# Attention, gated projection and product block on one core: the RMS root of the first five units by ScalarE's square root, reciprocal and two Newton steps

## The chip, the core and the metric

The kernel runs on one core of a Trainium2 chip. The metric is the device time of one execution in microseconds; three executions of the kernel before took 1012.33, 1013.52 and 1014.37 us, with a median of 1013.52.

## What is computed

Three blocks follow each other. Keys and values are averaged over eight positions each before the attention; the result is normalised by the root of its mean square, gated, and multiplied out; a second block multiplies two projections.

```
k_p, v_p = mean of k, v over 8 positions each          # batch 4, heads 8, seq 576, dim 64
attn = softmax(q @ k_p.T / sqrt(64));  x = attn @ v_p   # then 2304 tokens x 512
rms = sqrt(mean(x * x, axis=-1) + 1e-06)
xn  = x / rms * rms_g
x   = (silu(xn @ w_gate) * (xn @ w_val)) @ w_out        # d_ff 1536
out = ((x @ w_a) * (x @ w_b)) @ w_out2
```

The five weight matrices come in 64-bit floating point and are turned into 32-bit on the chip, by integer and bit instructions. Most products are made of three passes, of a high and a low part of each factor.

## The kernel before

The 2304 tokens are nine attention units of 256 tokens, 0 to 8. The first block runs over five tiles of 512, 256, 512, 512 and 512 tokens (TILES1); units 0 and 1 make the first tile, unit 2 the second, units 3 and 4 the third. While a tile is multiplied, the units of the next are worked on beside it. The order of the first two tiles' work is written out by hand (the tables FIRST and SECOND; a sign before a step says behind which work a step may stand), and a scheduler places the instructions of each engine in a queue that the engine then works in order. From the last tile on, the order is the program's own.

A unit's steps that matter here, with their lines:

- Scores: q is transposed (L298, copied by ScalarE at L307), multiplied by K (L318), and the maximum found and subtracted by VectorE (L327, L328). Two PSUM banks, tag "att", go round among these steps, so a step waits until the bank's last reader is done. Keys and values are pooled by VectorE (L189) or GpSimd (L180, L183) from tiles loaded at L169 and L171, two buffers.
- Values: the exponentials are transposed (L367, copied by ScalarE at L374) and multiplied by V (L420 for units 0 and 1, L399 for the others). ScalarE copies the result to x with the factor of the RMS weight (L423, L403), and squares it (L425, L406, L409).
- Mean square: TensorE sums the squares by a product with ones into a tile of 128x4 (L434 for units 0 and 1, L445 for 2 to 4).
- Root, `narrow_rsqrt` (L454), units 0 to 4: VectorE makes `a`, half the mean square, a first guess by integer operations (`start_newton`, L478 to L485), three Newton steps (L491 to L493), and a diagonal matrix of the 256 roots in two pieces (L464). TensorE spreads it by a product with ones (`spread`, L472, "rb" in the rows), VectorE scales x with it (L529). Units 5 to 8 use another path, with wide tiles at the same lines L478 to L493.
- Split: ScalarE casts x to its high part xh (L635), VectorE subtracts to the low part xl (L636).

The first block's 36 weight parts of 512 KB each are loaded by SyncE (L566, L571) into four staging tiles "st", converted by ScalarE (`begin`, L589 and L590), VectorE (`sign`, L596, L599) and GpSimd (`end`, L606), whose addition frees the staging tile; then split into wh by ScalarE (L620) and wl by GpSimd or VectorE (L621). The first tile's projections are L799, its Silu L807, its gated product L813, and the product with w_out L670. For the other tiles these are L649, L1239, L1247 and L670 or L662. Gates have one PSUM bank, values another.

Of the kernel before, what the change touches and what calls it, by code (L numbers as in the profile page):

```python
# [8 lines left out]
F32 = mybir.dt.float32  # L9
# [4 lines left out]
AF = mybir.ActivationFunctionType  # L14
ALU = mybir.AluOpType
AX = mybir.AxisListType

P = 128
# [45 lines left out]
def attention_moe_moe2(  # L64
# [14 lines left out]
    nc = tc.nc  # L79
    B, H, S, D = q.shape  # L80
    NT, DM = out.shape
# [19 lines left out]
    const = attn.enter_context(tc.tile_pool(name="const", bufs=1, side="right"))  # L101
# [10 lines left out]
    for t0, n in starts(TILES1):  # L112
        x2d[t0] = dr.tile([DM, n], F32, tag=f"x2_{t0}", name=f"x2_{t0}")

    ident = const.tile([P, P], F32, tag="ident", name="ident")
# [6 lines left out]
        out=mask, in_=mask, pattern=[[P, NV], [-SP, H]], compare_op=ALU.is_ge,  # L122
# [3 lines left out]
        out=mask, in_=mask, pattern=[[-P, NV], [SP, H]], compare_op=ALU.is_ge,  # L126
# [7 lines left out]
    vp = const.tile([P, NV, D], F32, tag="vp", name="vp")  # L134
    nc.gpsimd.memset(vp, 0.0)
    gneg = const.tile([P, KD], F32, tag="gneg", name="gneg")

    VH, VL, VM = {}, {}, {}

# [218 lines left out]
    def value_steps(u, dest):  # L358
        t0, n = u * UNIT, UNIT
        box, eT = {}, {}  # L360
# [81 lines left out]
        def sum_tokens():  # L442
            box["sums"] = att_bank(f"sq_{u}")
            for i in range(NS):
                nc.tensor.matmul(  # L445
                    box["sums"][:, 2 * i:2 * i + 2],
                    box["ss"][:, i * P:(i + 1) * P],
                    ones.bitcast(F32)[:, :2],
                    start=(i == 0),
                    stop=(i == NS - 1),  # L450
                )
            narrow_rsqrt()

        def narrow_rsqrt():  # L454
            m = 2 * NS
            a = sm_p.tile([P, m], F32, tag="ba", name=f"ba_{u}")
            r = sm_p.tile([P, m], F32, tag="br", name=f"br_{u}")
            y = sm_p.tile([P, m], F32, tag="by", name=f"by_{u}")
            start_newton(box["sums"][:, :m], a, r)
            for _ in range(3):  # L460
                newton_step(a, r, y)
            diag = sm_p.tile([P, n], F32, tag="nr", name=f"dg_{u}")
            for i in range(NS):
                nc.vector.tensor_scalar_mul(  # L464
                    diag[:, i * P:(i + 1) * P], ident, r[:, 2 * i:2 * i + 1]
                )
            box["diag"] = diag

        def spread():
# [7 lines left out]
        def start_newton(src, a, r):  # L477
            nc.vector.tensor_scalar(  # L478
                out=a, in0=src, scalar1=0.5 / DM, scalar2=0.5e-6, op0=ALU.mult, op1=ALU.add
            )  # L480
            nc.vector.tensor_scalar(
                out=r.bitcast(I32), in0=a.bitcast(I32), scalar1=1, scalar2=None,
                op0=ALU.logical_shift_right,
            )
            nc.vector.tensor_scalar(  # L485
                out=r.bitcast(I32), in0=r.bitcast(I32), scalar1=-1.0,
                scalar2=float(0x5F3759DF - 0x400000), op0=ALU.mult, op1=ALU.add,
            )

        def newton_step(a, r, y):  # L490
            nc.vector.tensor_mul(y, r, r)  # L491
            nc.vector.tensor_mul(y, y, a)
            nc.vector.scalar_tensor_tensor(  # L493
                out=r, in0=y, scalar=1.5, in1=r, op0=ALU.subtract, op1=ALU.mult
            )
# [37 lines left out]
        if u * UNIT < TILES1[0]:  # L533
            return steps + [narrow_rsqrt, scale]
# [663 lines left out]
    for idx, (ph, t0, n) in enumerate(work):  # L1198
# [26 lines left out]
        for f, cols, last, ahead, own in jobs:  # L1225
            m = cols.stop - cols.start
# [94 lines left out]
```

## Time and profile before

| what | value |
|---|---|
| profiled execution, its own time | 1014.52 us |
| its span, first to last instruction | 1012.8 us |
| mean granted TensorE clock | 0.990 |
| TensorE (PE) busy | 976.4 us, 96% |
| VectorE (DVE) busy | 610.0 us, 60% |
| ScalarE (ACT) busy | 452.0 us, 45% |
| GpSimd (POOL) busy | 402.9 us, 40% |
| activation table loads | 16, 1283 ns each |

Busy time is an average over stages: TensorE's idle time lies almost wholly before 130 us, where the weights are converted and the first tile is made. In the rows, PE is TensorE, PEld its weight loads, DVE VectorE, ACT ScalarE, POOL GpSimd and SPq SyncE's queue; L12 is line 12 of the kernel before, and "out<-in" names tiles of the program.

### The profile page before, as it was taken

How to read it: one execution, taken by the hardware profiler on the slowest of the kernel's cores; microseconds unless marked ns; L12 is line 12 of the kernel's file. 1: busy time of each engine (PE TensorE's matmuls, PEld its weight loads, DVE VectorE, ACT ScalarE, POOL GpSimd, SP SyncE). 2: the span in 40 equal slices, each digit the busy share in tenths (PEclk: the TensorE clock that was granted, in tenths of full speed). 3: DMA queues.
4: the chain of work that ended last, by engine and by line, in shares of the span. 5: the costliest groups of instructions: out<-in, count | busy, mean ns of one | idle time of the engine just before them, and what ended most of it. 6: DMA issues, size and time to landing. Idle time of an engine off the chain costs nothing.

```text
span 1012.8 us, 13575 instructions
## 1 busy us (share of the span) xinstructions
PE 976.4 (96%) x4920; PEld 842.3 (83%) x4920; DVE 610.0 (60%) x966; ACT 452.0 (45%) x849; POOL 402.9 (40%) x324
## 2 busy tenths in 40 slices
PE   4878999999999999999999999999999999999998
PEld 3766666789888888888888899999999999888886
DVE  6898966766636565566338669667766665232321
ACT  3854662454644445544445545443444344331211
POOL 6476673434343354344356701433443333410000
PEclk8799999999999999999999999999999999999999
DMA  8556543330100001000121143434434445643431
GB/s 230 159 167 206 171 130 107 115 89 1 43 11 11 1 30 34 1 1 1 42 62 43 42 148 130 131 125 146 147 125 136 126 136 184 193 146 116 146 112 67
DMA packets 82946, 101.55 MB, mean 100 GB/s; under 512 B 24128, under 2 KB 63296, under 8 KB 82880
## 3 DMA queue, kind: packets, MB, share of 16 engines
q1 hardware_dynamic: 82736, 100.55, 32.0%
q8 instruction: 39, 0.64, 0.3%
q14 instruction: 27, 0.22, 0.1%
q10 hardware_dynamic: 144, 0.13, 0.0%
HBM read 73.93 MB, written 26.74 MB: 99 GB/s over the span
## 4 chain that ended last, share of the span: by engine, by line
PE 81%; DVE 11%; DMA 3%; issue 2%; ACT 2%; SPq 0%; DVEq 0%; ACTq 0%
PE o L1120 15%; PE X L1019 14%; PE v L649 10%; PE g L649 10%; PE acc L662 9%; PE Y L1019 7%; PE acc L670 3%; PE Z L1019 3%; PE xT L399 2%; PE v L799 2%; PE g L799 1%; PE sc L318 1%; DVE wf L596 1%; DVE wf L599 1%; DVE kp L189 1%
## 5 line engine op out<-in xcount | busy, mean ns | idle before, releaser
L621 POOL TENSOR_TENSOR wl<-wf,wh 128x512 fp32r<-128x512 f32 x144 | 196.6, 1373 | 230.7 <-ACT wh L620 221.0
L620 ACT CAST wh<-wf 128x512 fp32r<-128x512 f32 x156 | 94.8, 619 | 70.2 <-PE v L649 30.2
L1098 DVE TENSOR_TENSOR hl<-hf,hh 128x768 fp32r<-128x768 f32 x36 | 34.5, 963 | 95.0 <-ACT hh L1097 95.0
L1120 PE MATMUL o<-woh,hl 128*128 128x512 f32 x216 | 85.8, 397 | 0.0
L1120 PE MATMUL o<-woh,hh 128*128 128x512 f32 x216 | 85.0, 394 | 0.0
L1120 PE MATMUL o<-wol,hh 128*128 128x512 f32 x216 | 84.7, 392 | 0.0
L606 POOL TENSOR_TENSOR w<-w,st 128x512 int32<-128x512 int32 x24 | 31.9, 1329 | 116.8 <-DVE w L599 115.6
L649 PE MATMUL v<-xh,wl 128*128 128x512 f32 (+1 forms) x192 | 72.6, 378 | 1.6 <-DVE ht L1247 1.6
L649 PE MATMUL g<-xh,wl 128*128 128x512 f32 (+1 forms) x192 | 72.4, 377 | 0.0
L649 PE MATMUL v<-xh,wh 128*128 128x512 f32 (+1 forms) x192 | 69.9, 364 | 0.0
L649 PE MATMUL v<-xl,wh 128*128 128x512 f32 (+1 forms) x192 | 69.8, 364 | 0.0
L649 PE MATMUL g<-xh,wh 128*128 128x512 f32 (+1 forms) x192 | 69.8, 364 | 0.0
L649 PE MATMUL g<-xl,wh 128*128 128x512 f32 (+1 forms) x192 | 69.8, 363 | 0.0
L1097 ACT CAST hh<-hf 128x768 fp32r<-128x768 f32 x36 | 29.8, 834 | 87.9 <-PE o L1120 81.5
L670 PE MATMUL acc<-ht,wf 128*128 128x256 f32 (+1 forms) x208 | 67.0, 463 | 1.7 <-DVE xf L529 1.3
L606 POOL TENSOR_TENSOR wf<-wf,st 128x512 int32<-128x512 int32 x36 | 52.9, 1475 | 38.2 <-DVE wf L599 16.6
L1247 DVE TENSOR_TENSOR ht<-ht,v 128x512 f32<-128x512 f32 (+1 forms) x48 | 29.6, 617 | 60.3 <-PE v L649 56.2
L1239 ACT ACTIVATE ht<-g 128x512 f32<-128x512 f32 (+1 forms) x48 | 26.1, 544 | 74.3 <-PE g L649 73.7
L1027 ACT COPY p<-X 128x384 f32<-128x384 f32 x36 | 17.2, 478 | 90.2 <-PE X L1019 90.2
L662 PE MATMUL acc<-hh,wl 128*128 128x512 f32 x144 | 56.4, 392 | 0.0
L662 PE MATMUL acc<-hl,wh 128*128 128x512 f32 x144 | 56.1, 390 | 0.0
L662 PE MATMUL acc<-hh,wh 128*128 128x512 f32 x144 | 56.1, 389 | 0.0
(210 smaller groups left out, 2704.5 us busy)
## 6 DMA issues: line engine op xcount, KB each, us to landing
hf<-h SPq DMA_DIRECT2D x36, 384.0 KB
st<-in_moe_w_out_dram SPq DMA_DIRECT2D x24, 512.0 KB
h<-u SPq DMA_DIRECT2D x36, 192.0 KB
h<-p SPq DMA_DIRECT2D x36, 192.0 KB
st<-in_moe_w_gate_dram SPq DMA_DIRECT2D x12, 512.0 KB
st<-in_moe_w_val_dram SPq DMA_DIRECT2D x12, 512.0 KB
st<-in_moe_w_a_dram SPq DMA_DIRECT2D x12, 512.0 KB
st<-in_moe_w_b_dram SPq DMA_DIRECT2D x12, 512.0 KB
```

The lines of the kernel that those rows point to most:

```text
L606: nc.gpsimd.tensor_tensor(out=bits, in0=bits, in1=low, op=ALU.add)
L620: nc.scalar.copy(wh, wf[ph, f, i])
L621: (nc.vector if boot["alt"] else nc.gpsimd).tensor_sub(wl, wf[ph, f, i], wh.bitcast(F32))
L649: nc.tensor.matmul(bank[:, :n], w[:, c, :], x[:, c, cols], start=(i == 0), stop=(i == 3 * KD - 1),)
L662: nc.tensor.matmul(accs[c][:, cols], w[:, c, :], x[:, :n], start=(f == 0 and i == 0 and cols.start == 0), stop=(f == NF - 1 and i == 2),)
L670: nc.tensor.matmul(accs[c][:, cols], wf[0, f, 2][:, c, :], ht[:, :cols.stop - cols.start], start=(f == 0 and cols.start == 0), stop=(f == ...
L799: nc.tensor.matmul(bank[:, :n], w[:, c, :], x[:, c, cols], start=(c == 0 and i == 0), stop=(c == KD - 1 and i == len(terms) - 1),)
L1019: nc.tensor.matmul(dst[:, :HALF], w[:, c0 + c, :], x[:, c, :], start=(start and i == 0), stop=(stop and i == 5), skip_group_check=True,)
L1097: nc.scalar.copy(hh, hf)
L1098: nc.vector.tensor_sub(hl, hf, hh.bitcast(F32))
L1120: nc.tensor.matmul(accs[i], x[:, sub], y, start=(f == 0 and j == 0), stop=(f == NF - 1 and j == 2),)
L1247: nc.vector.tensor_mul(ht[:, :m], ht[:, :m], vb[:, :m])
```

## The change

The start by integer operations and the first of three Newton steps go. ScalarE takes the square root of the mean square (with a constant tile for the 1e-6), VectorE its reciprocal, and two refining steps follow, of which the first is written with other signs. The diagonal is made by ScalarE. ScalarE needs the table of the square root for this, so it loads that table before the root and Silu's or the exponential's again after it.

```diff
@@ -134,6 +134,8 @@
     gneg = const.tile([P, KD], F32, tag="gneg", name="gneg")
+    eps = const.tile([P, 2], F32, tag="eps", name="eps")
+    nc.gpsimd.memset(eps, 1e-6)
@@ -456,14 +458,23 @@
             y = sm_p.tile([P, m], F32, tag="by", name=f"by_{u}")
-            start_newton(box["sums"][:, :m], a, r)
-            for _ in range(3):
-                newton_step(a, r, y)
+            src = box["sums"][:, :m]
+            nc.scalar.activation(out=y, in_=src, func=AF.Sqrt, scale=1.0 / DM, bias=eps[:, 0:1])
+            nc.vector.tensor_scalar(
+                out=a, in0=src, scalar1=0.5 / DM, scalar2=0.5e-6, op0=ALU.mult, op1=ALU.add
+            )
+            nc.vector.reciprocal(r, y)
+            nc.vector.tensor_mul(y, r, r)
+            nc.vector.scalar_tensor_tensor(
+                out=y, in0=y, scalar=-1.0, in1=a, op0=ALU.mult, op1=ALU.mult
+            )
+            nc.vector.scalar_tensor_tensor(
+                out=r, in0=y, scalar=1.5, in1=r, op0=ALU.add, op1=ALU.mult
+            )
+            newton_step(a, r, y)
             diag = sm_p.tile([P, n], F32, tag="nr", name=f"dg_{u}")
             for i in range(NS):
-                nc.vector.tensor_scalar_mul(
-                    diag[:, i * P:(i + 1) * P], ident, r[:, 2 * i:2 * i + 1]
-                )
+                nc.scalar.mul(diag[:, i * P:(i + 1) * P], ident, r[:, 2 * i:2 * i + 1])
             box["diag"] = diag
```

Since the scheduler places instructions anew, other work moves too. In the changed kernel, lines behind the edit are larger by 2 to 11 (L364 to L458 by 2, L470 and later by 11). Three places:

ScalarE's queue at unit 0's root and unit 1's squares, before (ef is the transposed exponential, xf x, sq a square, st_1_0 and st_1_1 staged weights):

```order
L374 COPY ef_0_367<-eT_0_364 128x256
L374 COPY ef_1_393<-eT_1_390 128x256
L374 COPY ef_2_411<-eT_2_408 128x256
L589 ACTIVATE wf_0_1_435<-st_1_0_246 128x512
L590 ACTIVATE st_1_0_246<-st_1_0_246 128x512
L423 ACTIVATE xf_296<-xT_0_414,gneg 128x256
L425 ACTIVATE sq_0_418<-xT_0_414 128x256
L374 COPY ef_3_423<-eT_3_420 128x256
L423 ACTIVATE xf_296<-xT_1_425,gneg 128x256
L374 COPY ef_4_450<-eT_4_447 64x256
L589 ACTIVATE wf_0_1_497<-st_1_1_274 128x512
```

and with the change:

```order
L376 COPY ef_0_369<-eT_0_366 128x256
L462 ACT_TABLE_LOAD
L462 ACTIVATE by_373<-sq_299,eps 128x4
L376 COPY ef_1_392<-eT_1_389 128x256
L376 COPY ef_2_410<-eT_2_407 128x256
L600 ACTIVATE wf_0_1_434<-st_1_0_248 128x512
L601 ACTIVATE st_1_0_248<-st_1_0_248 128x512
L425 ACTIVATE xf_298<-xT_0_413,gneg 128x256
L477 ACTIVATE dg_383<-ident,br_372 128x128 x2
L427 ACTIVATE sq_0_417<-xT_0_413 128x256
L376 COPY ef_3_422<-eT_3_419 128x256
L425 ACTIVATE xf_298<-xT_1_424,gneg 128x256
```

The load, the root and the diagonal stand between unit 1's copies and squares, and the begin of st_1_1 (wf_0_1_497 before) has moved behind all of unit 1's squares.

VectorE's queue at the end of unit 1's root, before (ba, br and by are the narrow tiles, wf weights under conversion, ht the gated product):

```order
L599 SCALAR_TENSOR_TENSOR wf_0_1_528<-st_1_2_356,wf_0_1_528 128x512
L493 SCALAR_TENSOR_TENSOR br_473<-by_474,br_473 128x4
L596 TENSOR_SCALAR wf_0_2_562<-wf_0_2_562 128x512
L491 TENSOR_TENSOR by_474<-br_473 128x4
L599 SCALAR_TENSOR_TENSOR wf_0_2_562<-st_2_0_433,wf_0_2_562 128x512
L492 TENSOR_TENSOR by_474<-by_474,ba_472 128x4
L493 SCALAR_TENSOR_TENSOR br_473<-by_474,br_473 128x4
L813 TENSOR_TENSOR ht<-ht,v 128x256
L491 TENSOR_TENSOR by_474<-br_473 128x4
L492 TENSOR_TENSOR by_474<-by_474,ba_472 128x4
L493 SCALAR_TENSOR_TENSOR br_473<-by_474,br_473 128x4
L464 TENSOR_SCALAR dg_487<-ident,br_473 128x128 x2
```

and with the change:

```order
L463 TENSOR_SCALAR ba_471<-sq_412 128x4
L466 RECIPROCAL br_472<-by_473 128x4
L467 TENSOR_TENSOR by_473<-br_472 128x4
L468 SCALAR_TENSOR_TENSOR by_473<-by_473,ba_471 128x4
L471 SCALAR_TENSOR_TENSOR br_472<-by_473,br_472 128x4
L502 TENSOR_TENSOR by_473<-br_472 128x4
L503 TENSOR_TENSOR by_473<-by_473,ba_471 128x4
L504 SCALAR_TENSOR_TENSOR br_472<-by_473,br_472 128x4
L824 TENSOR_TENSOR ht<-ht,v 128x256
L607 TENSOR_SCALAR wf_0_1_524<-wf_0_1_524 128x512
L540 TENSOR_TENSOR xf_298<-xf_298,rb_486 128x4x256
L610 SCALAR_TENSOR_TENSOR wf_0_1_524<-st_1_2_358,wf_0_1_524 128x512
```

The whole root stands in one piece, and the conversion of st_1_2 and st_2_0, which stood between its links, comes behind it.

VectorE's queue where unit 2 is scaled, before (kp and vp are pooled keys and values, m and e maximum and exponent of the scores, rb the spread root):

```order
L189 TENSOR_REDUCE kp_1593<-kv_4_1596 72x64 x2
L327 TENSOR_REDUCE m_1485<-sc_0_1488 128x4
L327 TENSOR_REDUCE m_1485<-sc_1_1493 128x4
L328 TENSOR_TENSOR e_1367<-sc_0_1488,m_1485 128x288
L328 TENSOR_TENSOR e_1367<-sc_1_1493,m_1485 128x288
L189 TENSOR_REDUCE kp_1593<-kv_3_1610 72x64
L529 TENSOR_TENSOR xf_1210<-xf_1210,rb_1510 128x4x256
```

and with the change:

```order
L191 TENSOR_REDUCE kp_1586<-kv_4_1589 72x64 x2
L191 TENSOR_REDUCE kp_1586<-kv_3_1603 72x64 x2
L329 TENSOR_REDUCE m_1478<-sc_0_1481 128x4
L329 TENSOR_REDUCE m_1478<-sc_1_1486 128x4
L330 TENSOR_TENSOR e_1363<-sc_0_1481,m_1478 128x288
L330 TENSOR_TENSOR e_1363<-sc_1_1486,m_1478 128x288
L824 TENSOR_TENSOR ht<-ht,v 128x512
L191 TENSOR_REDUCE vp<-kv_2_1608 128x64
L540 TENSOR_TENSOR xf_1206<-xf_1206,rb_1503 128x4x256
```

Both pools of kv_3 now stand ahead of the subtraction that frees the bank for the spread root, and the first pool of kv_2 ahead of the scaling.

## Rows read from the trace of the kernel before

**Rows 1.** Busy time by stage, core 0: stretch, length, engines, TensorE clock, DMA.

```profile
34.00:62.40 28.40, 21.16 (x106) 17.61 (x103) 25.12 (x49) 16.27 (x34) 16.28 (x14) 0.82 0.53 162
...
72.00:94.00 22.00, 17.82 (x68) 13.45 (x67) 21.80 (x24) 11.34 (x20) 17.79 (x14) 0.92 0.69 216
...
260.00:1012.80 752.80, 746.12 (x3730) 658.65 (x3728) 413.52 (x646) 317.08 (x591) 262.45 (x199) 1.00 0.28 89
```

**Rows 2.** Chain of waits, 0 to 80 us: start, length, engine, tile, line.

```profile
39.63 1.02 PE rb L472 x2
...
43.90 0.16 DVE ba L478
...
45.14 0.96 DVE kp L189
46.10 1.20 DVE xl L636 x2
...
47.38 0.33 DVE wf L596
...
54.17 0.04 DVE dg L464
...
57.55 1.14 DVE xf L529
...
59.37 3.03 DVE xl L636 x2
```

**Rows 3.** Who waited for whom, TensorE, whole span: total us, times, longest.

```profile
PE qT L298 <- DMA q<-in_q_dram: 10.5, 1, 10.5
PE v L799 <- DVE ht L813: 4.2, 2, 2.8
...
PE rb L472 <- DVE e L328: 1.0, 1, 1.0
```

**Rows 4.** VectorE, lines L492 and L341: duration ns minimum, median, maximum.

```profile
L492 DVE TENSOR_TENSOR by<-by,ba x15: 146/162/1211, 35.8 to 249.7; 128x4 f32<-128x4 f32 x15
...
L341 DVE RECIPROCAL sum<-sum x11: 184/239/253, 19.0 to 430.0; 128x16 f32<-128x16 f32 x7, 128x8 f32<-128x8 f32 x4
```

**Rows 5.** Instructions in order of time, ScalarE, 222 to 225 us: start, length.

```profile
222.71 1.28 ACT L1239 ACT_TABLE_LOAD   x1
224.01 0.38 ACT L1239 ACTIVATE ht<-g 128x256 f32<-128x256 f32 x1
```

**Rows 6.** ScalarE, line L403: duration ns minimum, median, maximum.

```profile
L403 ACT ACTIVATE xf<-xT,gneg x28: 467/474/489, 138.8 to 458.8; 128x256 f32<-128x256 f32 x28
```

**Rows 7.** Instructions in order of time, ScalarE, 24 to 70 us.

```profile
33.46 1.04 ACT L374 COPY ef<-eT 128x256 f32<-128x256 f32 x3
...
37.03 0.68 ACT L589 ACTIVATE wf<-st 128x512 f32<-128x512 f32 x1
...
43.04 1.14 ACT L635 CAST xh<-xf 128x512 fp32r<-128x512 f32 x2
```

**Rows 8.** Instructions in order of time, GpSimd, 24 to 70 us.

```profile
41.72 1.28 POOL L606 TENSOR_TENSOR wf<-wf,st 128x512 int32<-128x512 int32 x1 [3.08 <-ACT st L590]
...
66.71 1.37 POOL L606 TENSOR_TENSOR wf<-wf,st 128x512 int32<-128x512 int32 x1 [3.20 <-DVE wf L599]
```

**Rows 9.** SyncE's queue in order of time, 20 to 75 us.

```profile
43.03 0.34 SPq L571 DMA_DIRECT2D st<-in_moe_w_out_dram  x1
...
55.73 0.39 SPq L566 DMA_DIRECT2D st<-in_moe_w_val_dram  x1
```

**Rows 10.** Instructions in order of time, VectorE, 182 to 188 us.

```profile
184.14 0.68 DVE L636 TENSOR_TENSOR xl<-xf,xh 128x512 fp32r<-128x512 f32 x1
```

**Rows 11.** Instructions in order of time, ScalarE, 222 to 262 us.

```profile
241.35 0.38 ACT L1239 ACTIVATE ht<-g 128x256 f32<-128x256 f32 x1 [0.68 <-PE g L649]
...
249.16 0.39 ACT L1239 ACTIVATE ht<-g 128x256 f32<-128x256 f32 x1 [2.74 <-PE g L649]
```

**Rows 12.** Who waited for whom, 66 to 140 us.

```profile
ACT wf L589 <- DMA st<-in_moe_w_val_dram: 5.2, 3, 2.1
```

## Prediction

> **What bounds the kernel now.** I read the page's busy shares first (TensorE leads), then the busy time by stage, the chain of waits, and who waits for whom. Time is to be had only where TensorE isn't busy: the table by stage shows it busy for 746.12 of the last 752.8 us, but for only 21.16 of the 28.4 us from 34 to 62.4, with a mean granted clock of 0.82, and for 17.82 of 22 us from 72 to 94 [rows 1]. In both stretches VectorE is nearly full (25.12 of 28.4, 21.80 of 22). Units 0 and 1 lie in the first of them; units 2 to 4 lie where TensorE is nearly full.
>
> From 43.9 to 62.4 us the chain of waits runs almost wholly on VectorE: unit 1's root starts at 43.90, the low part of x for unit 0 is made at 46.10, unit 1's diagonal comes at 54.17, the scaling of its x at 57.55, and the low part of that is whole at 62.4 [rows 2]. So some fourteen instructions on tiny tiles, spread through VectorE's queue, hold up half of the first tile for 10.3 us. Besides, TensorE waits 4.2 us for gated products that stand behind the weights' conversion in that queue, and 1.0 us, in unit 2, for an attention subtraction [rows 3].
>
> **The change part by part.** *VectorE.* Per unit, three start instructions, nine of Newton's and two diagonal ones go (14); one affine, one reciprocal and six products come (8). A small one takes 0.16 us at the median but up to 1.2, the reciprocal of a similar tile 0.18 to 0.25 [rows 4]; in the stretch at hand the long ones lie beside a GpSimd instruction and end with it. I take 0.2 each with the gap to the next, so twelve links (2.4 us) become eight (1.6), without the blocks. What stands between the links counts for more: the order rows show unit 1's links now in one piece.
>
> *ScalarE.* Per unit a square root and two diagonal instructions come, and seven table loads in all (one for units 0 and 1 together, two each for units 2, 3 and 4). A load takes 1.28 us, and the Silu after it starts 0.02 later [rows 5], so 1.3 each and 9.1 in all. The Trainium skill, page "ScalarE: Activation LUTs", section "What ACT_TABLE_LOAD costs", gives 2.66 us for a switch, load and drain. These rows show no such drain; by the page unit 0 would come 1.4 us later than below and the sum would be -2.4 instead of -3.8. The root and the diagonal have no row on ScalarE; below them lies 0.31 (the pitch of its copies of 256 columns [rows 7]) or less, above them 0.47, its copy with a scale from a tile [rows 6]. With fewer columns than either, I take 0.25 for four and 0.3 for 128.
>
> *Unit 0.* The root's table load stands behind the first of three score copies, which start at 33.46 [rows 7]: 33.8 + 1.3 + 0.25 = 35.35. On VectorE seven links and a conversion step of 0.33 to 0.4 [rows 2] follow: 37.2. Diagonal 0.6: 37.8; TensorE's spread 1.02 and the scaling 1.14 [rows 2]: 40.0, where they end at 41.9 now. ScalarE casts x at 40.4 instead of 43.04 [rows 7]. VectorE pools two K chunks at about 1.0 each [rows 2] and starts the low part at 42.1 instead of 46.10: -4.0.
>
> *Unit 1.* Its last sums of squares now stand behind twelve projections: 45.4, which is 1.5 later than now. Root 45.7; the chain 1.6 and one GpSimd instruction of up to 1.3 beside it: 47.3 to 48.6, I take 48. Silu's table load and Silu end at 47.4, before the chain does, and so cost nothing; were the root later they would add up to 1.7. Diagonal, spread and scaling end at 50.7 instead of 58.7; the cast waits for two conversion pairs on ScalarE (51.4), and the low part is whole at 53.1 instead of 62.4: -9.3.
>
> *Weights.* These pay for it. ScalarE's part of the weight that it begins at 37.03 now [rows 7] moves behind unit 1's squares, to 42.2; VectorE's and GpSimd's follow, so the addition of 41.72 [rows 8] comes at 45.2. Each addition frees one of four staging tiles, so the load that SyncE issues at 43.03 [rows 9] goes out at 46.5; the one of 55.73 at about 59.5, since in SyncE's queue a V load that waits for a K pooling now stands ahead of it. But these were early: the tile loaded at 43.03 is added only at 66.71 [rows 8], because VectorE was in arrears. Following VectorE's new queue, that addition comes at about 61, and the three after it 4 to 5 us before their present places. From there the four staging tiles pace the conversion as they do now.
>
> TensorE can get ahead only by the smaller of 9.3 (x) and 4 to 5 (weights): I take **-4.5** for the start. The rest of the 9.3 becomes new waiting for weights at 60 to 75.
>
> *Units 2 to 4.* In unit 2 the pools of two more K chunks stand ahead of the subtraction that TensorE's spread waits for (1.0 now [rows 3]), and a V pool ahead of the scaling. VectorE's low part ends at 184.8 now [rows 10]; with the two pools ahead it comes at 186.9, some 0.2 after TensorE needs it, and the spread waits 1.6 instead of 1.0: together **+0.7**. In unit 3 two loads and the wait for the diagonal make the Silu of 241.35 [rows 11] about 0.6 late, and delayed copies hold a PSUM bank: 0 to +0.6; I take 0, since the product that needs this Silu comes four microseconds later. In unit 4 two loads and the root (2.85) meet ScalarE's idle 2.74 before the Silu of 249.16 [rows 11]: 0. What VectorE saves there brings nothing, as TensorE doesn't wait for it. The fill of a 128x2 tile by GpSimd at the program's start is hidden by the 10.5 us in which TensorE waits for the first q [rows 3]; without that cover it is below an addition's 1.28 [rows 8].
>
> Sum: -4.5 + 0.7 = **-3.8 us**. The profiled execution took 1014.52 (span 1012.8 and 1.7 around it), so 1010.7; it lies 1.0 above the median of 1013.52, and against the median this is **1009.7**.
>
> **The rivals.**
> *The gain is twice that.* If the weights keep up, TensorE follows x: -9.3, of which unit 2 takes 0.7 and waits on gated products some 1.1: 1006. For it: VectorE, which converts the weights, is relieved too, and gated products move ahead of conversion steps in its queue (4.2 us of waits [rows 3]). Against: VectorE's 21.80 of 22 us from 72 to 94 [rows 1].
> *Nothing is left.* ScalarE, working in order, is the new wait: in units 3 and 4 Silu stands behind a load, a root, a diagonal that VectorE must finish first, and another load. If the chain there meets GpSimd's instructions as the long ones do now (1.2 instead of 0.16 [rows 4], twice), each Silu comes 1.5 to 2 us late, and TensorE, with one bank for gates, stops for it: +3 to +4 on the -3.8, so 1013. Beside this stands the rule of the same page, section "Table sets: the hidden batching unit", to group calls by set, which the change goes against. Against it: ScalarE's idle 2.74 [rows 11].
> *Slower.* The staging ring decides. If TensorE's path up to 94 us is set not by VectorE's arrears but by when the four tiles come free, the 3.5 us by which the load of 43.03 slips pass through every later load: 1013.5 + 3.5 = 1017. It decides from the point where ScalarE waits for a load longer than VectorE works off its queue. For it: ScalarE does wait for weight loads between 66 and 140 [rows 12]. Against: the tile loaded at 43.03 lies until 66.71 [rows 8, 9].
> *The clock.* A mean of 0.82 over 28.4 us [rows 1] is 10 us at the lower level of 1.2 GHz. If TensorE's waiting for unit 1 keeps it there 10 us longer, the matmuls at 53 to 63 take up to twice their time; since weights bind until about 70, that is 2 us of the gain at most, inside the forecast's own bounds.
>
> **How the numbers follow.** Forecast 0.50, twice the gain 0.17, nothing left 0.21, slower 0.12. About 0.2% (2 us) is what a measurement of this kernel can tell from no change. By its bounds (start -3 to -6, units 2 to 4 from 0 to +2) the forecast runs from 1007 to 1012.5, and a tenth of it lies within 0.2%. Faster: 0.45 + 0.17 = 0.62; same: 0.05 + 0.20 = 0.25; slower: 0.12 and 0.01 of the third case, 0.13. The range that holds 8 in 10 takes in the upper half of the double gain and the case of nothing left: 1005 to 1014.5.
>
> **What would show it.** Right: unit 1's diagonal at about 48 instead of 54, the low part of its x whole near 53, 23 table loads of 1.28 with nothing behind them, the addition of 66.71 near 61, TensorE busier from 34 to 62, and the stretch after 260 as long as now. Wrong: VectorE idle after 46 for want of loads (the staging ring), TensorE waiting for Silu near 240 and 250 (ScalarE), or the addition at 66 or later.

## The result and the profile after

The changed kernel takes 1021.66 us (median of 5 runs, 1017.75 to 1023.55) where the kernel before takes 1013.52: the ratio is 1.0073, with an interval of [1.0059, 1.0088]. It is slower by 7.4 us by the ratio and by 8.1 by the medians, where 3.8 us less was forecast, and it lies above the range. The ratios, here and below, leave out two executions that lie far off all others (1956 us in E1, 1565 us of the kernel before). The profiled execution took 1021.66, its span is 1019.6 and its mean granted clock 0.986. Profiles are compared below with the one of the kernel before, which lies 1.0 above its median, so they show the loss some 1 us too small.

Busy time by stage, the changed kernel, columns as in [rows 1]; the last row is the end, as long as that of [rows 1]:

```profile
34.00:62.40 28.40, 23.11 (x122) 19.24 (x121) 20.52 (x37) 19.91 (x43) 12.82 (x12) 0.82 0.41 126
72.00:94.00 22.00, 16.71 (x67) 13.23 (x67) 21.05 (x23) 13.15 (x23) 17.72 (x13) 0.84 0.69 222
225.00:270.00 45.00, 41.66 (x258) 36.89 (x257) 21.56 (x42) 26.82 (x57) 16.05 (x12) 0.96 0.04 13
267.00:1019.60 752.60, 746.36 (x3730) 658.69 (x3728) 415.23 (x646) 316.85 (x591) 262.68 (x199) 1.00 0.28 88
```

From 34 to 62.4 VectorE's busy time fell from 25.12 to 20.52 as it should, but TensorE is idle in a place where it never was: between 225 and 270. The kernel before in the same stretch:

```profile
225.00:270.00 45.00, 45.00 (x290) 40.23 (x289) 28.01 (x66) 22.39 (x50) 19.18 (x14) 1.00 0.09 25
```

TensorE's own milestones say where the time went. Its sums for unit 2 start at 161.31 instead of 159.26 (+2.0), those for unit 3 at 235.11 instead of 233.89 (+1.2), the spread of unit 4 at 260.78 instead of 253.98 (+6.8), and the end of the span is 6.8 later. So **5.6 of the 6.8 us arise between unit 3's sums and unit 4's spread**, and the start, which was to bring 4.5, loses one or two. The two ends of this stretch, before:

```profile
233.89 0.50 PE L445 MATMUL sq<-ones,ss 128*128 128x2 f32 x4
...
253.98 0.59 PE L472 MATMUL rb<-dg,ones 128*128 128x256 f32 x2
```

and with the change:

```profile
235.11 0.50 PE L447 MATMUL sq<-ones,ss 128*128 128x2 f32 x4
...
260.78 0.70 PE L483 MATMUL rb<-dg,ones 128*128 128x256 f32 x2 [0.29 <-ACT dg L477]
```

**Units 3 and 4.** Who waited for whom, TensorE, 225 to 268 us (total, times, longest). In the kernel before, this list has one wait of 0.4.

```profile
PE xT L401 <- ACT ss L408: 2.2, 1, 2.2
PE sq L447 <- DVE ss L412: 0.9, 1, 0.9
PE rb L483 <- ACT dg L477: 0.3, 1, 0.3
```

ScalarE in order of time, where these waits come from:

```profile
235.31 0.38 ACT L1250 ACTIVATE ht<-g 128x256 f32<-128x256 f32 x1 [1.06 <-PE g L660]
235.71 1.28 ACT L462 ACT_TABLE_LOAD   x1
237.01 0.26 ACT L462 ACTIVATE by<-sq,eps 128x4 f32<-128x4 f32 x1
237.41 0.37 ACT L376 COPY ef<-eT 128x256 f32<-128x256 f32 x1
237.68 1.14 ACT L631 CAST wh<-wf 128x512 fp32r<-128x512 f32 x2
241.12 0.69 ACT L477 ACTIVATE dg<-ident,br 128x128 f32<-128x128 f32 x2 [2.30 <-DVE br L504]
241.72 0.45 ACT L405 ACTIVATE xf<-xT,gneg 128x256 f32<-128x256 f32 x1
242.07 0.37 ACT L408 ACTIVATE ss<-xT 128x256 f32<-128x256 f32 x1
```

and VectorE at the same time:

```profile
237.26 0.42 DVE L1258 TENSOR_TENSOR ht<-ht,v 128x256 f32<-128x256 f32 x1 [5.16 <-ACT by L462]
237.60 0.15 DVE L463 TENSOR_SCALAR ba<-sq 128x4 f32<-128x4 f32 x1
...
238.47 1.20 DVE L502 TENSOR_TENSOR by<-br 128x4 f32<-128x4 f32 x1
239.70 1.19 DVE L503 TENSOR_TENSOR by<-by,ba 128x4 f32<-128x4 f32 x1
```

The diagonal of unit 3 stands in ScalarE's queue ahead of the scaled copy and the square of unit 4's first product with V. ScalarE reaches it at 238.8 and sits idle for 2.30 us, since VectorE's chain is not done: two links took 1.2 instead of 0.16, beside two GpSimd instructions that ScalarE's casts of 237.68 had just released (GpSimd in order of time):

```profile
238.38 2.49 POOL L632 TENSOR_TENSOR wl<-wf,wh 128x512 fp32r<-128x512 f32 x2 [4.26 <-ACT wh L631]
```

Long links are not new: before, the chain had two as well (1.13 and 1.21, at 235.23 and 236.79). New is that ScalarE stands behind the chain. The copy and the square (241.72, 242.07) could have run in that time; until they have, they hold one of the two "att" banks. TensorE at that place:

```profile
242.49 1.16 PE L401 MATMUL xT<-ef,vm 128*128 128x128 f32 x8 [2.16 <-ACT ss L408]
...
243.73 0.34 PE L660 MATMUL g<-xh,wl 128*128 128x256 f32 x1
243.87 0.41 PE L660 MATMUL g<-xh,wh 128*128 128x256 f32 x1
244.09 0.42 PE L660 MATMUL g<-xl,wh 128*128 128x256 f32 x1
```

After the wait of 2.16 the products come 0.21 to 0.22 apart instead of 0.12 to 0.14: the granted clock is 0.95 from 242 to 244, 0.50 to 246 and 0.69 to 248. Of two levels, 1.2 and 2.4 GHz, that is 0.2 + 2.0 + 1.2 = 3.4 us at the lower one, in which half is lost: 1.7 us. With the three waits (2.2, 0.9, 0.3) this makes 5.1 of the 5.6.

**The start.** VectorE and TensorE at unit 0's root:

```profile
36.16 0.16 DVE L463 TENSOR_SCALAR ba<-sq 128x4 f32<-128x4 f32 x1 [1.88 <-ACT by L462]
```

```profile
36.38 4.63 PE L422 MATMUL xT<-ef,vm 128*128 128x256 f32 x10 [1.36 <-DVE ba L463]
41.02 1.06 PE L483 MATMUL rb<-dg,ones 128*128 128x256 f32 x2
```

VectorE's affine needs only the sums, but waits for ScalarE's root, which reads the same PSUM tile: the two readers come one after the other. The Trainium skill, page "PSUM — Partial Sum Buffer", section "PSUM bank collisions raise a hardware error", asks software to keep two engines' accesses to one bank apart, reads by ScalarE and VectorE included; the trace agrees, with 1.88 us. TensorE then waits 1.36 for this bank ("acc3"), into which unit 1's product with V goes, does ten products at the lower clock (0.56 from 35 to 40), and comes to unit 0's spread at 41.02 instead of 39.63 [rows 2]. The staging loads, answering to [rows 9]:

```profile
49.96 0.35 SPq L582 DMA_DIRECT2D st<-in_moe_w_out_dram  x1
57.90 0.37 SPq L577 DMA_DIRECT2D st<-in_moe_w_gate_dram  x1
63.37 0.37 SPq L577 DMA_DIRECT2D st<-in_moe_w_val_dram  x1
```

The load of 43.03 goes out at 49.96, that of 55.73 at 63.37. Below these two are called the third and the fifth load, counted from the load of 35.56 before and of 35.72 with the change.

### The profile page after: what moved, and what is told of

It is laid out like the page before. It is cut to its first block, busy times and chain, and to the rows that moved or that the text cites. A ratio compares the mean times of both kernels' runs of the same rounds, so it can differ in the third digit from the quotient of the medians.

```text
span 1019.6 us, 13567 instructions
## 1 busy us (share of the span) xinstructions
PE 979.4 (96%) x4920; PEld 844.4 (83%) x4920; DVE 606.3 (59%) x936; ACT 465.0 (46%) x871; POOL 405.3 (40%) x325
## 5 line engine op out<-in xcount | busy, mean ns | idle before, releaser
L632 POOL TENSOR_TENSOR wl<-wf,wh 128x512 fp32r<-128x512 f32 x144 | 198.8, 1388 | 237.6 <-ACT wh L631 227.9
```

What stands on the lines that cost most here:

```text
L632: (nc.vector if boot["alt"] else nc.gpsimd).tensor_sub(wl, wf[ph, f, i], wh.bitcast(F32))
```

## The experiments

**Theory**: the loss is ScalarE's in-order wait at units 3 and 4; the start is about even. **Rivals**: the seven table loads cost by their number; the staging ring passes the late loads on. In the diffs `seed` and `diag`, as sets, stand for the units that have the new root and ScalarE's diagonal; the other units keep the code of before.

```diff
-            <the new root>
+            if u in seed:
+                <the new root>
+            else:
+                start_newton(box["sums"][:, :m], a, r)
+                for _ in range(3):
+                    newton_step(a, r, y)
...
-                nc.scalar.mul(diag[:, i * P:(i + 1) * P], ident, r[:, 2 * i:2 * i + 1])
+                if u in diag: nc.scalar.mul(...)
+                else: nc.vector.tensor_scalar_mul(...)
```

### Units 3 and 4

**E1, units 0 and 1 only.**

```diff
+ seed = (0, 1); diag = (0, 1)
```

> New root and ScalarE's diagonal in units 0 and 1 only; units 2 to 4 as in the kernel before. Theory (most of the loss, 5.7 of 6.8 us, arises at units 3 and 4, where ScalarE stands in order behind VectorE's chain; the start costs the rest, 2.7 us at 95 us and 1.2 by 227 us): 1 to 3 us slower than before, ratio 1.001 to 1.003. Rival 'staging ring' (late weight loads pass through the whole first tile): the start keeps all that was lost, 4 to 8 us, ratio 1.004 to 1.008. Rival 'number of table loads' (each of the seven costs the same): one load, about 1 us.

Measured: 1012.79 us against 1013.2, ratio 0.9996 [0.9985, 1.0008]: the same as before. The stretch from unit 3's sums to unit 4's spread is 20.1 us, as before. So units 0 and 1 together bring no loss.

**E2, units 3 and 4 only.**

```diff
+ seed = (3, 4); diag = (3, 4)
```

> New root and ScalarE's diagonal in units 3 and 4 only; units 0 to 2 as in the kernel before. Theory: 5 to 6 us slower than before, ratio 1.005 to 1.006, with TensorE's wait of some 2 us for unit 3's transposed exponential times V behind ScalarE's square, and a lower granted clock just after it near 240 us. Rival 'staging ring': no weights are loaded there, so no loss, within 1 us. Rival 'number of table loads': four of the seven, 4 us slower.

Measured: 1017.93, ratio 1.0041 [1.0028, 1.0054]; the profiled execution is 4.4 us longer than before's. TensorE's wait is there to the tenth, the granted clock behind it is 0.84, 0.50 and 0.81 from 240 to 246, and the stretch is 25.65 us:

```profile
PE xT L401 <- ACT ss L408: 2.2, 1, 2.2
PE sq L447 <- DVE ss L412: 0.9, 1, 0.9
PE rb L493 <- ACT dg L483: 0.3, 1, 0.3
```

A staging ring can't cause this. The ratio is a little under what was expected, and four table loads at 1.3 would give as much; so the diagonal and the loads have to be told apart.

**E3, all units, diagonal by VectorE.**

```diff
+ seed = (0, 1, 2, 3, 4); diag = ()
```

> As the changed kernel, with square root and seven table loads in all five units, but the diagonal made by VectorE as before. Theory (it is the diagonal's place in ScalarE's queue, where squares and copies stand behind VectorE's chain, that costs the 5.7 us): units 3 and 4 lose 0 to 2 us, so 1 to 4.5 us slower than before, ratio 1.001 to 1.0045. Rival 'table loads': nothing is regained, 7 to 8 us slower than before.

Measured: 1016.9, ratio 1.0032 [1.0019, 1.0044]. The wait for the square is gone, the clock stays at 1.00, and the stretch is 21.6 us, 1.5 over before, with all table loads in place:

```profile
PE sq L447 <- DVE ss L412: 0.9, 1, 0.9
PE rb L493 <- DVE dg L485: 0.2, 1, 0.2
```

VectorE's chain has the two long links here too:

```profile
236.50 1.21 DVE L512 TENSOR_TENSOR by<-br 128x4 f32<-128x4 f32 x1
237.75 1.20 DVE L513 TENSOR_TENSOR by<-by,ba 128x4 f32<-128x4 f32 x1
```

So the long links alone don't make TensorE wait for the square; they do so where ScalarE waits for them.

**E4, root taken from VectorE's affine.** (`zero` is a tile of zeros.)

```diff
-            nc.scalar.activation(out=y, in_=src, func=AF.Sqrt, scale=1.0 / DM, bias=eps[:, 0:1])
             nc.vector.tensor_scalar(
                 out=a, in0=src, scalar1=0.5 / DM, scalar2=0.5e-6, op0=ALU.mult, op1=ALU.add
             )
+            nc.scalar.activation(out=y, in_=a, func=AF.Sqrt, scale=2.0, bias=zero[:, 0:1])
```

> As the changed kernel, but VectorE's affine reads the sums first and ScalarE takes the root of twice its result, so that the sums' PSUM bank is free after VectorE's one instruction; in ScalarE's queue unit 0's diagonal then comes behind two copies of unit 1, and unit 3's diagonal behind the copy and square that free the attention bank. Theory: unit 1's product with V starts near 34.5 us instead of 36.4, the 2.2 us wait at 242 us goes, so 0 to 4 us slower than before, ratio 1.000 to 1.004. Rival 'table loads' or 'staging ring': as the changed kernel, 7 to 8 us slower than before.

Measured: 1015.13, ratio 1.0017 [1.0009, 1.0026]. Unit 1's product starts at 34.7, and the stretch is 21.7 us. ScalarE in order of time; the copy and the square now stand ahead of the diagonal, whose wait of 1.04 holds no bank:

```profile
235.14 0.47 ACT L406 ACTIVATE xf<-xT,gneg 128x256 f32<-128x256 f32 x1
235.51 0.38 ACT L409 ACTIVATE ss<-xT 128x256 f32<-128x256 f32 x1
236.93 0.69 ACT L484 ACTIVATE dg<-ident,br 128x128 f32<-128x128 f32 x2 [1.04 <-DVE br L515]
```

The diagonal is still on ScalarE, in another place; the root's source differs too, and VectorE's chain has one long link instead of two. Together with E3 this says that the place costs the larger part.

**E6, ScalarE's diagonal without the new root.**

```diff
+ seed = (); diag = (0, 1, 2, 3, 4)
```

> Old root with integer seed and three Newton steps in all five units, no root and no table load added, but the diagonal made by ScalarE. Theory: the diagonal's place in ScalarE's queue costs by itself; unit 3's stands ahead of the scaled copy and the square that free the attention bank, so TensorE waits there 0.5 to 2 us, and the stretch of units 3 and 4 is 1 to 4 us longer than before; total 1 to 4 us slower, ratio 1.001 to 1.004. Rival 'table loads': no loss, within 1 us of before, and TensorE waits for no square near 240 us.

Measured: 1018.32, ratio 1.0056 [1.0041, 1.0070], more than expected. No table load was added, and TensorE still waits:

```profile
PE xT L401 <- ACT ss L408: 1.4, 1, 1.4
PE xT L401 <- ACT ef L376: 0.3, 1, 0.3
```

After a wait of 1.4 the clock stays at 1.00 here, and the stretch is 21.8 us, +1.7. The rest lies ahead of it: unit 1's diagonal comes at 57.71 instead of 54.17, and unit 2's sums at 161.77, 2.5 late.

**E5, the changed kernel again.**

```diff
 (no edit)
```

> The changed kernel once more, for a second profile and more times. Up to 60 us its program equals that of the run with units 0 and 1 alone, instruction for instruction, yet its profile had TensorE at the lower clock from 35 to 43 us and the spread of unit 0 at 41.0 instead of 38.3. Theory (the start loses nothing by its order, only by where the lower clock falls; the loss of 5.6 us lies at units 3 and 4): the distance from unit 3's sums to unit 4's spread is again 25.6 to 25.8 us whatever the clock of the start, and executions whose mean granted clock is 0.991 or more take 1016 to 1018.5 us, those of 0.986 or less 1021 to 1024. Rival 'staging ring': the start is late in every execution, unit 0's spread at 40.5 to 41.5 and the K transpose near 101 us again.

Measured: 1019.07, ratio 1.0062 [1.0044, 1.0081]; the profiled one is 1019.0 at 0.993. The stretch is 25.7 us again, with the same waits. The start isn't: unit 0's spread is at 38.76, unit 2's sums at 158.31, 3.0 us before those of the first profile, from the same program. Windows of 5 us, columns as in [rows 1], first profile of the changed kernel:

```profile
35.00:40.00 5.00, 3.64 (x10) 2.90 (x10) 2.12 (x10) 4.28 (x11) 1.98 (x2) 0.56 0.57 179
40.00:45.00 5.00, 5.00 (x26) 4.08 (x25) 2.88 (x3) 2.90 (x9) 0.00 (x0) 0.76 0.51 152
```

and the second:

```profile
35.00:40.00 5.00, 3.66 (x19) 3.14 (x20) 2.63 (x11) 4.99 (x14) 2.02 (x2) 1.00 0.57 171
40.00:45.00 5.00, 4.36 (x29) 3.57 (x28) 4.42 (x7) 4.16 (x10) 0.46 (x1) 1.00 0.81 218
```

Both have the wait of 1.36; the ten products after it take 4.63 and 2.43 us. In the second profile:

```profile
36.34 2.43 PE L422 MATMUL xT<-ef,vm 128*128 128x256 f32 x10 [1.36 <-DVE ba L463]
```

The boundaries that were expected by clock held only roughly: 1015.85 to 1019.0 at 0.993 and 0.994, 1019.15 and 1019.71 at 0.987 and 0.988, 1022.88 at 0.985. So the loss at the start isn't the same in every execution, and 3 us between the two profiles go with the clock.

| kernel | stretch, us | TensorE's waits in it | clock |
|---|---|---|---|
| before; E1 | 20.1 | none over 0.4 | 1.00 |
| changed; E5; E2 | 25.7; 25.7; 25.65 | 2.2, 0.9, 0.3 | falls |
| E3 (diagonal by VectorE) | 21.6 | 0.9, 0.2 | 1.00 |
| E4 (diagonal behind the square) | 21.7 | 0.9, 0.3 | 1.00 |
| E6 (diagonal alone) | 21.8 | 1.4, 0.3 | 1.00 |

Root and table loads cost 1.5 of the 5.6 (E3), and the diagonal on ScalarE adds 4.1. Of these, 1.7 come with the diagonal alone (E6); the other 2.4 come only when the later root and the diagonal's place meet: then the wait is 2.2 instead of 1.4, and the clock falls, which is put at 1.7 above. The number of table loads doesn't decide, since E6 without one loses as much here as E3 with four.

The parts don't add up to the whole: by the ratios E1 and E2 lose 3.8 us together, the changed kernel 7.4 and 6.3 (E5). No run has the new root in unit 2 alone. From unit 2's sums to unit 3's the changed kernel is no longer than E1 and E2 (73.8 and 74.0 us), so the rest lies ahead of unit 2's sums or in the spread between executions, and stays open.

### The start

**E10, unit 0 only**, and **E7, unit 1 only.**

```diff
+ E10: seed = (0,); diag = (0,)
+ E7:  seed = (1,); diag = (1,)
```

> New root and ScalarE's diagonal in unit 0 only. Theory (unit 1 brings the gain, unit 0 a loss by the conversion steps that slip behind it): 1 to 4 us slower than before, ratio 1.001 to 1.004. Rival (both units gain, and what was lost in the run with both is an interplay): 0 to 3 us faster.

> New root and ScalarE's diagonal in unit 1 only. Theory: the gain of the start is unit 1's chain in one piece (its x whole 4 to 6 us earlier), and unit 0's part brings a wait of 1.4 us of TensorE for the bank of the sums; without that, and with the second part of weight 1 begun ahead of unit 1's squares as in the kernel before, the weights keep up better: 1 to 4 us faster than before, ratio 0.996 to 0.999. Rival (the weights' pace from 70 us on is the same whatever unit 1 does): within 1 us of before.

Measured: E10 1015.16, ratio 1.0021 [1.0011, 1.0031], slower; E7 1009.35, ratio 0.9969 [0.9958, 0.9981], faster. Unit 1's chain in E7, VectorE in order of time:

```profile
45.87 0.16 DVE L464 TENSOR_SCALAR ba<-sq 128x4 f32<-128x4 f32 x1
...
46.91 0.69 DVE L620 SCALAR_TENSOR_TENSOR wf<-st,wf 128x512 int32<-128x512 int32 x1
47.52 0.15 DVE L512 TENSOR_TENSOR by<-br 128x4 f32<-128x4 f32 x1
47.71 0.16 DVE L513 TENSOR_TENSOR by<-by,ba 128x4 f32<-128x4 f32 x1
47.90 0.16 DVE L514 SCALAR_TENSOR_TENSOR br<-by,br 128x4 f32<-128x4 f32 x1
```

It takes 2.2 us, since GpSimd does nothing beside it, and is done at 48.06, where the prediction had it with unit 0's root as well. In the changed kernel the chain begins at 48.04 and four links are long (0.40, 1.21, 1.20 and 0.57); its diagonal comes at 52.28.

**E11, unit 1 only, diagonal by VectorE.**

```diff
+ seed = (1,); diag = ()
```

> New root in unit 1 only, with its diagonal by VectorE as before. Theory (the gain is VectorE's chain in one piece, and ScalarE comes to the diagonal without waiting in unit 1): the same gain as with ScalarE's diagonal, 2 to 4.5 us faster than before, ratio 0.9955 to 0.998. Rival (the diagonal on ScalarE is part of the gain): 0 to 2 us faster.

Measured: **1008.46, ratio 0.9957 [0.9945, 0.9968]**: faster than both kernels, and the best of the study. What ScalarE gives unit 1 is the root; its diagonal is no part of the gain.

**E8, units 0 and 1, root from the affine.** (E4's edit, in units 0 and 1.)

```diff
+ seed = (0, 1); diag = (0, 1)
+            nc.scalar.activation(out=y, in_=a, func=AF.Sqrt, scale=2.0, bias=zero[:, 0:1])
```

> New root and ScalarE's diagonal in units 0 and 1 only, with the root taken from VectorE's affine so that the sums' bank is free at once. Theory: unit 1's product with V starts near 34.5 us instead of 35.9, no wait for the bank; 0 to 2 us faster than before, ratio 0.998 to 1.000, as the table load now stands nearer to unit 0's chain. Rival (this wait is what keeps the start from gaining): 3 to 5 us faster.

Measured: 1014.73, ratio 1.0019 [1.0010, 1.0028]. TensorE's wait for the bank is gone, and nothing is won: neither expectation held. The third load still goes out at 47.6.

**E9 and E12, units 0 and 1, conversions brought forward** in the table FIRST ("c" is a conversion step).

```diff
 E9
-... =V0.6 =V0.7@v =V1.1@g -x0! -g0a V1.2@att,acc3 =V1.3@acc2,acc1 c =g0b
+... =V0.6 c =V0.7@v =V1.1@g -x0! -g0a V1.2@att,acc3 =V1.3@acc2,acc1 =g0b
 E12
-=V0.5@att -c =V1.0@acc0 =V0.6 =V0.7@v =V1.1@g -x0! -g0a V1.2@att,acc3 =V1.3@acc2,acc1 c =g0b
+=V0.5@att -c c =V1.0@acc0 =V0.6 =V0.7@v =V1.1@g -x0! -g0a V1.2@att,acc3 c =V1.3@acc2,acc1 =g0b
...
-... =V1.7@acc0 s0.1! =c =x1 ...
+... =V1.7@acc0 s0.1! =x1 ...
```

> New root and ScalarE's diagonal in units 0 and 1, and in the first tile's hand-written order one conversion step moved ahead of unit 0's product with V and unit 1's, so that ScalarE begins the first and second parts of weight 1 ahead of unit 1's squares. Theory (unit 0's new root gains nothing because it sets the conversion back; staging loads then go out as early as with unit 1 alone): the loads of 47.2 and 54.7 us go out at 43 to 44 and 49 to 52, the K transpose comes at 94 to 97.5 us, 1 to 4 us faster than before, ratio 0.996 to 0.999. Rival (unit 0's root itself, the bank of the sums that waits for ScalarE, costs the gain): within 1 us of before, as with units 0 and 1 before this step was moved.

> New root and ScalarE's diagonal in units 0 and 1, with the conversion of the first part of weight 1 placed ahead of unit 0's root and that of the second, both of ScalarE's instructions, ahead of unit 1's first copy; the run with one step moved had brought only one of the two forward, and its third load still went out at 46.6 us. Theory (unit 0's new root gains nothing because it sets the conversion back): the third and fourth loads go out at 41 to 44 and 47 to 51 us, and the kernel is 1 to 4 us faster than before, ratio 0.996 to 0.999. Rival (unit 0's root costs by TensorE's wait for the bank and the lower clock behind it, whatever the weights do): the loads are early, and the time is within 1 us of before or longer.

Measured: E9 1015.43, ratio 1.0028 [1.0018, 1.0037], with the third load still at 46.6, so that its condition wasn't met. E12 1015.95, ratio 1.0031 [1.0020, 1.0042]: the third load goes out at 40.6, but the fourth at 51.7 and the fifth at 59.7, because ScalarE stands 3.4 us before unit 1's diagonal with the next begins behind it. In both, TensorE has a new wait of 3.2 and 4.1 us for K pooled by GpSimd.

**E13 and E14, unit 1's diagonal off ScalarE.** (E14 has E12's edit of FIRST.)

```diff
+ E13: seed = (0, 1); diag = (0,)
+ E14: seed = (0, 1); diag = ()
```

> New root in units 0 and 1, unit 0's diagonal on ScalarE, unit 1's on VectorE; up to unit 1's diagonal all queues are as in the run with units 0 and 1. If ScalarE's in-order wait for unit 1's chain (2.6 us, with two begins of weight parts behind it) is what takes the start's gain: the begins that came at 50.1 and 51.7 us come 2 us or more earlier, the fourth load goes out at 51 to 53 us instead of 54.7, and the kernel is 1.5 to 4 us faster than before, ratio 0.996 to 0.9985. If the loads are late by unit 0's root itself: the third load still goes out at about 47 us, and the time is within 1.5 us of before.

> New root in units 0 and 1, both diagonals on VectorE, and both first conversions of weight 1 brought forward as in the run with both parts first. If late weights are what takes the gain, by whichever way: the third load goes out at 40 to 42 us, the fourth at 46 to 50, the fifth at 50 to 56 (before: 43.0, 50.7, 55.7), and the kernel is 2 to 5 us faster than before, ratio 0.995 to 0.998. If unit 0's root costs by something else on TensorE's own path (the bank of the sums, the clock behind it, unit 1's products behind twelve projections): within 1.5 us of before or slower, although the loads are early.

Measured: E13 1014.15, ratio 1.0007 [0.9994, 1.0020], the third load at 49.6; so, by the time measured, ScalarE's wait at unit 1's diagonal isn't what takes the gain. The late load says less: the profiled execution had TensorE at a clock of 0.52 from 35 to 40 us, and unit 0's spread at 40.72 instead of E1's 38.33, ahead of the edit. E14 1016.99, ratio 1.0040 [1.0025, 1.0055], with early loads (40.8, 51.2, 53.6) but a late x, since conversions again stand between the links of unit 1's chain, and the same wait for pooled K:

```profile
52.39 0.38 PE L212 MATMUL kT<-ident,kp 72*128 72x72 f32 x1 [3.83 <-POOL kp L185]
```

| kernel | new root in | low part of unit 1's x whole | third, fourth, fifth load | unit 2's sums | ratio |
|---|---|---|---|---|---|
| before | none | 62.4 | 43.0, 50.7, 55.7 | 159.3 | 1 |
| E11 | 1 | 53.2 | 42.2, 49.0, 55.3 | 153.1 | 0.9957 |
| E7 | 1 | 54.6 | 43.5, 51.3, 56.8 | 154.7 | 0.9969 |
| E1 | 0, 1 | 56.9 | 47.2, 54.7, 60.2 | 157.5 | 0.9996 |
| E13 | 0, 1 | 59.6 | 49.6, 57.4, 62.9 | 160.8 | 1.0007 |
| E8 | 0, 1 | 57.8 | 47.6, 55.5, 61.0 | 159.0 | 1.0019 |
| E9 | 0, 1 | 61.0 | 46.6, 52.3, 59.8 | 160.0 | 1.0028 |
| E10 | 0 | 62.9 | 47.8, 53.8, 59.0 | 159.8 | 1.0021 |
| E12 | 0, 1 | 61.9 | 40.6, 51.7, 59.7 | 161.9 | 1.0031 |
| E14 | 0, 1 | 62.2 | 40.8, 51.2, 53.6 | 160.9 | 1.0040 |

Times in a row are those of one profiled execution, and two of the same program were 3.0 us apart at unit 2's sums (E5), so the ratio decides. By it the kernel gains only where x is early and the loads are less than 1.2 us late (E7, E11). That both are needed fits the ratios, but no run changed one of the two alone, so it is argued and not shown; in E1's profile unit 2's sums come 1.8 early although its loads are 4 us late. What unit 0's new root costs (2.1 us by itself) stays open: its bank wait (E8), ScalarE's wait for unit 1 (E13) and the third load (E12) were each taken away, and the gain of unit 1 didn't come back; E9, E12 and E14 also brought a wait of their own.

## Why the prediction was wrong

The forecast was -3.8 us, and the changed kernel's first profile is 6.8 longer than before's. Of the 10.6 us between these two figures 5.6 arise in units 3 and 4 and 5.0 ahead of them: two steps of the sum failed, the 0 for unit 3 and the -4.5 for the start. (By its own terms the forecast's lower bound is 1007.5, not 1007; nothing hangs on it.)

- **Small costs: right.** 23 table loads of 1.28; the root starts 0.02 after its load ends (235.71, 237.01). The Trainium skill, page "ScalarE: Activation LUTs", section "What ACT_TABLE_LOAD costs", adds a drain to each load; the trace shows nothing like it here. The root takes 0.26 (taken 0.25), two diagonals 0.69 (0.6), a link 0.16.
- **Unit 3, "0 to +0.6; I take 0": the first step that failed.** It looked at Silu and at the product that needs it. What TensorE waited for was the bank that the "delayed copies hold", named in the same sentence and not followed into ScalarE's queue: the copy and the square stand behind the diagonal. Measured +4.1 for this, of which 1.7 is put down to the clock (E2, E3, E4).
- **Unit 4, 0:** the table loads and the root cost 1.5 over both units (E3); TensorE's waits of 0.9 and 0.2 to 0.3 are there with either diagonal.
- **Unit 0, -4.0: wrong in its first link.** The affine was taken to run beside the root. It waits for it, and TensorE for its bank; the low part starts at 45.18 (43.23 in E5) and not at 42.1.
- **Unit 1, -9.3: a quarter to a half.** Its low part is whole at 60.1 (58.0 in E5, 56.9 in E1), not at 53.1: the chain began 2 us late and took 4.1 us instead of 2.3, since GpSimd's instructions lay beside four of its links and not beside one. Where it met none (E7, E11) x came at 54.6 and 53.2.
- **Weights.** The third load was put at 46.5 and came at 49.96 (47.9 in E5); the addition of 66.71 [rows 8] was to come at 61 and came second in a pair that starts at 67.34. "These were early" was wrong: the slack was used up by the slip. TensorE's wait for gated products, which stand behind the conversion, is 7.3 us instead of 4.2 [rows 3]. That TensorE gains the smaller of x and weights fits the ratios, but isn't shown.
- **Start, -4.5: the second step that failed,** by the three lines above: between +2 and -1 came in its place (unit 2's sums in the two profiles). -3.1 and -4.4 us are what unit 1 alone gives (E7, E11); that the last is near -4.5 is chance, as unit 0's part is missing from it. Why unit 0's root takes this gain away is not known.
- **Unit 2, +0.7:** nothing; from its sums to unit 3's it is 74.6 us before and 73.8 after, and its spread waits 1.0 us for VectorE in both, not 1.6.
- **The rivals.** "Nothing is left" had half of the mechanism, ScalarE in order behind a chain that meets GpSimd, with 3 to 4 us where 5.6 came; but it had TensorE wait for Silu, where it waited for the square, and it counted on a start that wasn't there. "Slower" had the late loads, and part of the slip is passed on: the ninth load goes out at 75.75 instead of 72.22 (73.61 in E5, 72.55 in E1). That is at most the +2.0 at unit 2, and 1.2 of it is left at unit 3; E2 has the larger loss without it. "The clock", at most 2, was 3.0 at the start in one profile of two and 1.7 at units 3 and 4.

## What to carry to other kernels

When work moves to another engine, look at what stands behind it in that engine's queue and which buffers that holds: here two tiny diagonals kept a square from freeing a PSUM bank, and the same diagonals one place later (E4) cost no such wait. When two engines read one tile in PSUM, look at what waits for its bank: here VectorE waited 1.88 us for ScalarE, and TensorE 1.36 for VectorE. Letting ScalarE work from VectorE's result took TensorE's wait away, but in E8 it brought no time. And try a change unit by unit: by the ratios the same edit is worth -3.1 us in unit 1, +2.1 in unit 0 and +4.2 in units 3 and 4. These don't add up to the whole, so the sum of parts has to be measured too.

## What was not expected of the hardware

The same program, after the same wait of 1.36 us, had TensorE at 1.2 GHz from about 36 us in one profile and at 2.4 GHz in another, and was 3 us apart at unit 2's sums. Among the other runs with this wait, 35 to 40 us had a clock of 1.00 in E1 and 0.52 in E13. After waits of 2.16 or 2.17 us for unit 3's square the clock fell in all three profiles that have them (changed, E5, E2); after 1.4 in E6 it didn't. What decides in between no run here shows.
